# A token mixer behind linear attention: three groups of transfers moved in the program

## The chip, the cores and the metric

The kernel runs on one core of one Trainium2 chip. The metric is device time in microseconds (us), the median of five runs. Beside it there is one profiled execution, whose trace gives each instruction's start and length on each engine: TensorE (PE; PEld is its loading of weights), VectorE (DVE), ScalarE (ACT), GpSimd (POOL), and SyncE (SP), which only issues transfers.

## The reference

For each of 8 batches, 8 heads, 576 tokens and head size 64:

```
phi(x) = elu(x) + 1
kv  = phi(k)^T v                      # 64 x 64 for each head
x   = phi(q) kv / (phi(q) . sum(phi(k)) + 1e-6)     # heads side by side: 576 x 512
h   = relu(x^T w_tok1) w_tok2         # mixes the tokens: 512 x 576
u   = x + h^T
out = u + relu(u w_ch1) w_ch2         # mixes the channels: 512 -> 1536 -> 512
```

Inputs and output are float32; the products run on bf16 operands.

## The kernel before

A batch's 576 tokens are four tiles of 128 and a tail of 64. The tails of two batches (an even one and the odd one after it) are worked on together. The main loop works in blocks: block n does the channel mixer of batch n on TensorE (mm3 against w_ch1 at L543, then w_ch2) and, in between, everything that batch n + 1 and n + 2 need: phi of q and k, kv, the attention quotient (nd_all, L261), mm1 and mm2 of the token mixer.

The order on every engine is the program's own order; no scheduler changes it. Each block has a list `big` of TensorE steps and a list `fill` of other work, each with the number of the step behind which it is put: `put(24, phi_end, "k", 3, 2, 2)` puts this work behind step 24. Entries of one number keep the order in which they were put. An engine carries out its own instructions in that order and waits at each for what it needs, so an instruction that waits holds up all behind it on the same engine.

The names that matter here:

- `phi_exp`, `phi_add`, `phi_end` (L151, L157, L165): exp on ScalarE; max(x + 1, 1), called y, on VectorE; then their minimum on VectorE into `qp` or `kp`. Each runs twice for a batch, on half of the heads.
- `qtr_dma` (L219 to 223): SyncE transposes `qp` into `qT` with two transposing transfers, one for each half of the partitions. `utr_dma` (L519) does it for two tiles of `u` at a time, `utr_tail_dma` for the tails. `live["crossbar"]` remembers the last such transfer of q or u.
- `mm2a`, `mm2b` (L325): the second product of the token mixer for tiles 0, 1 and for 2, 3. VectorE adds x (L337); that is u. `uta` and `utb` are the two transfers that transpose u into uT.
- `load_all(n, nms, gate)` (L916): SyncE loads of a batch. With a gate, the first load waits until the given transfer has landed.
- `kv` (L191, then copies on ScalarE at L197).
- The product with w_ch2 is one step of Strassen's scheme in Winograd's form: seven products of half the size (`pair_product`, L854; in the last block `product`, L768, and `tail_product`, L823 for the pair of tails), with sums of rows beforehand (`row_sums`, L655) and sums of results in PSUM. `pair_end` (L863) reads a result and adds u. `mix_one` (L712) does the same to a part of mm3; its results pass an add and relu on VectorE (L531). `pair_copy` (L859) keeps a partial result on ScalarE. `mm4` for the tails (L583) is direct.
- `group_sums` (L700) and `u_sums` (L689) are the sums of weights and of uT for these schemes; `mm4_end` (L610) reads the result of a pair of tails.
- `last_block` follows a string `SEQUENCE`: `p61` is product 6 of half j = 1 with its read, `P61` the product alone, `R61` the read alone; `t6` is product 6 of the tails with its read, `T` and `U` product and read alone; `s` are the tails' row sums on GpSimd. Reads are L778 and, for the tails, L833.

Outputs leave through obuf. In the blocks before the last, GpSimd issues them (L869, and L612 for tails). In the last block SyncE and ScalarE do: the second half j = 1 in quarters of 64 KB for each issue (L798), the first half j = 0 in two issues of 256 KB when its last quarter is done (L801), the tails in four issues of 128 KB (L837), two of which are GpSimd's.

There are eight semaphores for the transfers that SyncE and ScalarE issue, used in turn; an issue first waits until the last transfer on its semaphore has landed. In the last block the two engines issue alternately, so that is the transfer four places back on the same engine.

Of the kernel before, what the change touches and what calls it, by code (L numbers as in the profile page):

```python
# [19 lines left out]
def kernel(  # L20
# [20 lines left out]
    nc = tc.nc  # L41

    B, H, S, D = q.shape
# [3 lines left out]
    R = 4  # L47
# [66 lines left out]
    half = [slice(0, 64), slice(64, 128)]  # L114
# [28 lines left out]
    def o_slots(m):  # L143
        at = o_at[0] if o_at[0] + m <= 8 else 0
        o_at[0] = (at + m) % 8
        return obuf[:, at:at + m]
# [69 lines left out]
        for h, ts in enumerate(TS):  # L216
            qtr_put(n, c, ts, tp[:, h], put)

    def qtr_dma(n):  # L219
        for a in range(2):  # L220
            live["crossbar"] = nc.sync.dma_start_transpose(
                out=qT[n % 2][:, 2 * TD * a:2 * TD * (a + 1)].rearrange("p (f s) -> p f s", s=D),
                in_=qp[half[a]].rearrange("p c t i d -> p (c t i d)"))
# [365 lines left out]
    outv = out.rearrange("n (p t) d -> n p t d", t=T)  # L589
# [163 lines left out]
    HC = [slice(0, 256), slice(256, 512)]  # L753
# [17 lines left out]
    def product_read(n, j, i):  # L771
        b = n % 2
        ps = live[{2: "Z", 5: "Y", 3: "Y"}.get(i, "X"), j]
        if i == 1:
            live["oj", j] = o_slots(2)
        o = live["oj", j]
        ur = lambda e, c: u[b][:, 2 * j + e, HC[c]]
        add = lambda e, c, x_, y_: nc.vector.tensor_tensor(out=o[:, e, HC[c]], in0=x_, in1=y_,  # L778
                                                           op=ALU.add)
        if i == 1:  # L780
            add(0, 0, ps, ur(0, 0))
        elif i == 2:
            add(0, 0, ps, o[:, 0, HC[0]])
        elif i == 6:
            add(0, 1, ps, ur(0, 1))
        elif i == 5:
            add(1, 1, ps, ur(1, 1))
        elif i == 7:
            add(1, 1, ps, o[:, 1, HC[1]])
        elif i == 4:  # L790
            add(1, 0, ps, ur(1, 0))
        elif i == 3:
            add(0, 1, ps, o[:, 0, HC[1]])
        queues = [nc.sync, nc.scalar]
        if j == 1 and i in (2, 7, 3, 4):
            d, cs = {2: (0, HC[0]), 7: (1, HC[1]), 3: (0, HC[1]), 4: (1, HC[0])}[i]
            for e in range(2):
                queues[e].dma_start(out=outv[n, :, 2 * (2 * j + d) + e, cs], in_=o[half[e], d, cs])  # L798
        elif i == 4:
            for e in range(2):  # L800
                queues[e].dma_start(out=outv[n, :, 4 * j + e:4 * j + e + 3:2], in_=o[half[e]])  # L801

# [21 lines left out]
    def tail_read(i):  # L826
        ps = live["t", {1: 2, 2: 7, 5: 3, 3: 3}.get(i, 2)]
        if i == 1:
            live["ot"] = o_slots(2)
        o = live["ot"]  # L830
        e, c, x_ = {1: (0, 0, ut[0]), 2: (0, 0, None), 6: (0, 1, ut[0]), 5: (1, 1, ut[1]),
                    7: (1, 1, None), 4: (1, 0, ut[1]), 3: (0, 1, None)}[i]
        nc.vector.tensor_tensor(out=o[:, e, HC[c]], in0=ps,  # L833
                                in1=o[:, e, HC[c]] if x_ is None else x_[:, HC[c]], op=ALU.add)
        if i in (3, 4):
            for b, queue in enumerate((nc.sync, nc.scalar) if e else (nc.gpsimd, nc.gpsimd)):
                queue.dma_start(out=outv[B - 4 + 2 * e + b, :, 2 * R], in_=o[half[b], e])  # L837


    ORDER = [1, 2, 6, 5, 7, 3, 4]  # L840
# [26 lines left out]
    def pair_put(n):  # L867
# [6 lines left out]

    SEQUENCE = """m01 m02 m11 m05 m15 m06 m12 c0 m21 m03 m16 m07 c1 m25 m13 m22 m17 m04 c2 m26 m14
        m23 c3 m27 r0 c4 m24 r2 c5 T10 T20 T11 T21 r4 s P10 R10 P20 P11 P50 U1 U2 R11 P60 R60
        P21 R50 P70 R20 R70 P51 R21 R51 p30 p61 p40 t6 t5 p71 t7 t3 t4 p31 p41"""

    def last_block(n):
        for e in SEQUENCE.split():  # L880
# [246 lines left out]
    put = lambda s, fn, *a: fill.append((s, lambda: fn(*a)))  # L1127
# [33 lines left out]
    put(19, todo["mm2a"])  # L1161
    put(19, todo["uta"])
    put(20, pair_copy, 1)
    put(20, phi_end, "k", 3, 0, 2)
    put(22, pair_copy, 2)
    put(22, phi_exp, "k", 3, 2, 2)
    put(22, vcast, 3, 1)
    put(24, phi_end, "k", 3, 2, 2)
    put(24, pair_end, 1, "X", 1, 1, 2)
    put(24, todo["mm2b"])  # L1170
    put(24, todo["utb"])
    put(24, pair_end, 1, "Z", 0, 0, 0)
    put(27, lambda: load_all(4, "qkv", live["crossbar"]))
    put(26, pair_end, 1, "Y", 0, 1, 1)
    put(28, pair_end, 1, "X", 1, 0)
    put(28, pair_put, 1)
    put(28, group_sums)
    put(28, kv, 3, range(2))
    run(big, sorted(fill, key=lambda e: e[0]))

    MIXED = (2, 3, 4, 5, 6)
    for n in range(2, B - 1):
        p, b = divmod(n, 2)
        tail = int(n == 3)
        mix = n in MIXED
        big = (m3x if mix else m3)(n) + m3t * tail + m4s(n) + m4(p, [8]) * tail
        b0 = 12 + 3 * tail
        todo = dict(steps(n + 1))
        fill = []
        put = lambda s, fn, *a: fill.append((s, lambda: fn(*a)))  # L1190
        at = lambda s, *nms: [put(s, todo.pop(nm)) for nm in nms if nm in todo]

        def phi_at(nm, ex, ad, en):
            for g in range(2):
                if ex is not None:
                    put(ex[g], phi_exp, nm, n + 2, 2 * g, 2)
            for g in range(2):
                put(ad[g], phi_add, nm, n + 2, 2 * g, 2)
                put(en[g], phi_end, nm, n + 2, 2 * g, 2)

        at(1, "nd")
        if mix and 3 < n < B - 2:
            for which in (3, 4):
                put(2, u_sums, which, tuc, b)
        if n + 2 < B:
            if n > 3:
                phi_at("k", None, (2, 2), (3, 4))
                put(5, load_all, n + 3, "k")
            nm = "k" if n == 3 else "q"
            if n > 3:  # L1210
                phi_at(nm, (7, 7), (10, 10), (16, 16))
            else:
                for which in (3, 4):
                    put(3, u_sums, which, tuc, b)
                for g in range(2):
                    put(3, phi_add, nm, n + 2, 2 * g, 2)
                    put(7, phi_exp, nm, n + 2, 2 * g, 2)
            put(16 if n > 3 else 10,
                *((qtr_dma, n + 2) if n != 3 else (load_all, n + 3, "k")))
            if n == 2:  # L1220
                for g in range(2):
                    put(13, phi_add, "k", n + 2, 2 * g, 2)
        at(7, "mm1")
        for s, k0 in ((7, 0), (11, 3)):
            for w in (1, 2):
                put(s, row_sums, n, w, k0, 3)
        if n < 4:
            for g in range(2):
                put(7 + 2 * g, phi_end, nm, n + 2, 2 * g, 2)
        if mix:  # L1230
            for which in (1, 2):
                put(0, u_sums, which, tuc, b)
        if n == 3:
            phi_at("q", (12, 13), (13, 13), (14, 14))
            put(15, qtr_dma, n + 2)
        at(13, "mm2a", "uta")
        put(14, row_sums, n, 3, 0, KH)
        put(b0 + 1, pair_copy, 0)
        if n == 2:
            for g in range(2):  # L1240
                put(b0 + 1, phi_exp, "k", n + 2, 2 * g, 2)
                put(b0 + 2, phi_end, "k", n + 2, 2 * g, 2)
            put(b0 + 4, load_all, n + 3, "k")
        at(b0 + 3 - tail, "mm2b", "utb")
        put(b0 + 4 - tail, row_sums, n, 4, 0, KH)
        put(b0 + 4 - tail, pair_end, n, "Z", 0, 0, 0)
        put(b0 + 5, pair_copy, 1)
        if n + 2 < B:
            for g in range(2):
                put(b0 + (5 if n == 2 else 2) + g, vcast, n + 2, g)  # L1250
        if n != 2:
            put(b0 + 7, lambda: load_all(n + 3, "qv", live["crossbar"] if n > 3 else None))
        put(b0 + 7, pair_copy, 2)
        if n > 2 and n + 3 < B:
            put(b0 + 8, k_exp, n + 3)
        put(b0 + 9, pair_end, n, "X", 1, 1, 2)
        if n == B - 2:
            at(b0 + 6, "mm2t", "utt")
        at(b0 + 9, "mm2t")
        if n + 2 < B:  # L1260
            put(b0 + 9, kv, n + 2, range(2))
        at(b0 + 9, "utt")
        if n == 2:
            put(b0 + 9, load_all, n + 3, "qv")
        put(b0 + 11, pair_end, n, "Y", 0, 1, 1)
        if n == B - 2:
            for which in (3, 4):
                put(3, u_sums, which, tuc, b)
            put(1, first_sum)
            for which in range(1, 5):  # L1270
                if which > 1:
                    put((3, 3, b0 + 2)[which - 2], first_sums, which)
                put(b0 + 10, u_sums, which)
        else:
            put(b0 + 13, pair_end, n, "X", 1, 0)
            put(b0 + 13, pair_put, n)
        assert not todo, todo
        run(big, sorted(fill, key=lambda e: e[0]))
# [31 lines left out]
```

## Time and profile before

| | |
|---|---|
| time, median of 5 runs | 250.85 us (248.11 to 251.35) |
| profiled execution | 251.13 us, of which the span from the first to the last instruction is 249.4 us |
| granted TensorE clock | 0.998 |
| PE busy | 236.6 us (95%) |
| DVE busy | 197.5 us (79%) |
| ACT busy | 139.3 us (56%) |
| POOL busy | 78.5 us (31%) |
| HBM read, written | 35.85 MB, 9.44 MB |

The profile names a group of instructions by the line of the program and what it writes and reads. "Busy" leaves out waiting and issuing. A row of waits reads: who waited, at which line, for whom, then the sum in us, how many times, and the longest. The chain of work that ended last is followed from the last instruction back to what released it. A stretch's row in a table of windows gives the stretch, its length, each engine's busy time with the number of its instructions, the granted clock, the share of the transfer engines that was busy, and GB/s.

### The profile page before, as it was taken

The page shows a single profiled execution, that of the slowest core. Times are in us where ns is not written, and L with a number is a line of the kernel's source. Part 1 is how long each engine was busy: PE and PEld are TensorE (multiplying, and loading weights), DVE is VectorE, ACT ScalarE, POOL GpSimd, SP SyncE. Part 2 cuts the span into 40 slices and gives each one's busy share as a digit, 9 for nine tenths or more (in the row PEclk, how much of TensorE's full clock was granted, in tenths as well). Part 3 has the DMA queues.
Part 4 walks back from the last instruction along what each step waited for, and adds up shares of the span by engine and source line. Part 5 has one row for each costly group of instructions (what it writes and reads, how often), then busy time and mean ns, then how long its engine had stood idle before and what let it go on. Part 6 is the DMA issues. An engine that isn't in the chain of part 4 may idle for free.

```text
span 249.4 us, 6065 instructions
## 1 busy us (share of the span) xinstructions
PE 236.6 (95%) x2476; PEld 162.2 (65%) x2496; DVE 197.5 (79%) x349; ACT 139.3 (56%) x224; POOL 78.5 (31%) x90
## 2 busy tenths in 40 slices
PE   7799999999999898989999999999999999999992
PEld 3484455554877455755688556775677566888881
DVE  5954878897999768997995489978996879956862
ACT  4764791579765276735897168556853651266000
POOL 9770030496504500062002600061006700520551
PEclk9999999999999999999999999999999999999999
DMA  6999999999525699669948975357929702361045
GB/s 247 266 203 258 359 260 335 329 277 300 226 54 114 125 315 355 141 175 355 345 142 139 356 257 189 65 119 257 314 51 131 168 3 42 63 135 36 3 103 152
DMA packets 49708, 48.40 MB, mean 194 GB/s; under 512 B 30032, under 2 KB 35536, under 8 KB 49680
## 3 DMA queue, kind: packets, MB, share of 16 engines
q1 hardware_dynamic: 41568, 34.87, 46.6%
q0 software_dynamic: 7568, 12.49, 22.9%
q10 hardware_dynamic: 544, 0.66, 0.9%
q8 instruction: 19, 0.31, 0.5%
q14 instruction: 9, 0.07, 0.1%
HBM read 35.85 MB, written 9.44 MB: 182 GB/s over the span
## 4 chain that ended last, share of the span: by engine, by line
PE 53%; DMA 8%; DVE 7%; issue 2%; DVEq 0%
PE ps L854 15%; PE ps L543 12%; PE ps L712 5%; DMA q_raw<-in_q_dram 4%; DMA uT<-u 4%; PE ps L740 4%; PE ps L768 4%; PE ps L312 3%; PE ps L325 3%; PE ps L570 2%; PE ps L823 2%; DVE u L337 1%; PE ps L261 1%; DVE v_raw L655 1%; DVE y L157 1%
## 5 line engine op out<-in xcount | busy, mean ns | idle before, releaser
L543 PE MATMUL ps<-uT,wc 128*128 128x512 bf16 x252 | 60.2, 379 | 2.1 <-DMA uT<-u 1.8
L550 ACT ACTIVATE cr<-ps 128x512 bf16<-128x512 f32 x59 | 34.5, 600 | 34.6 <-PE ps L543 34.5
L543 PEld LDWEIGHTS <-wc 128*128 128x128 bf16 x256 | 24.0, 98 | 26.8 <-DMA uT<-u 2.5
L865 POOL TENSOR_TENSOR obuf<-obuf,q_raw 128x512 f32<-128x512 f32 x6 | 7.6, 1269 | 96.7 <-DVE obuf L863 63.2
L854 PE MATMUL ps<-k_raw,v_raw 128*128 128x256 bf16 x216 | 24.9, 273 | 0.0
L854 PEld LDWEIGHTS <-cr 128*128 128x128 bf16 x216 | 20.9, 98 | 5.2 <-DVE cr L531 1.5
L854 PEld LDWEIGHTS <-v_raw 128*128 128x128 bf16 x216 | 21.1, 98 | 3.9 <-issue 0.4
L151 ACT ACTIVATE e<-q_raw 128x1152 bf16<-128x1152 f32 x16 | 18.5, 1163 | 8.3 <-DVE den L241 5.2
L863 DVE TENSOR_TENSOR obuf<-ps,u 128x512 f32<-128x512 f32 x24 | 16.1, 685 | 7.2 <-PE ps L854 5.0
L151 ACT ACTIVATE e<-k_raw 128x1152 bf16<-128x1152 f32 x16 | 18.2, 1165 | 3.5 <-DMA k_raw<-in_k_dram 3.5
L854 PE MATMUL ps<-wc,cr 128*128 128x256 bf16 x144 | 17.9, 273 | 1.2 <-DVE cr L531 1.2
L276 DVE TENSOR_TENSOR x<-ps,dens 128x768 bf16<-128x768 f32 x18 | 17.2, 954 | 0.4
L655 DVE TENSOR_TENSOR v_raw<-cr 128x768 bf16<-128x768 bf16 (+2 forms) x24 | 14.8, 617 | 1.6 <-ACT cr L718 1.6
L337 DVE TENSOR_TENSOR u<-ps,x 128x1024 bf16<-128x1024 f32 x12 | 14.6, 1219 | 0.7 <-PE ps L325 0.3
L157 DVE TENSOR_SCALAR y<-q_raw 128x1152 bf16<-128x1152 f32 x16 | 11.9, 767 | 2.9 <-DMA q_raw<-in_q_dram 2.9
L176 ACT CAST vs<-v_raw 128x1152 bf16<-128x1152 f32 x12 | 13.5, 1161 | 0.0
L157 DVE TENSOR_SCALAR y<-k_raw 128x1152 bf16<-128x1152 f32 x16 | 11.7, 763 | 2.1 <-DMA k_raw<-in_k_dram 2.1
L312 PE MATMUL ps<-x,w 128*128 128x512 bf16 x49 | 13.0, 379 | 0.3
L165 DVE TENSOR_TENSOR qp<-e,y 128x1152 bf16<-128x1152 bf16 x16 | 11.7, 753 | 0.9 <-ACT e L151 0.6
L865 POOL TENSOR_TENSOR obuf<-obuf,part 128x512 f32<-128x512 f32 x6 | 7.6, 1271 | 14.3 <-DVE obuf L863 14.3
L325 PE MATMUL ps<-ar,w2p 128*128 128x512 bf16 x44 | 11.8, 379 | 0.3
L583 PE MATMUL ps<-wc,cr 128*128 128x512 bf16 x47 | 11.8, 379 | 0.2 <-DMA wc<-in_moe_w_ch_dram 0.2
(183 smaller groups left out, 465.9 us busy)
## 6 DMA issues: line engine op xcount, KB each, us to landing
k_raw<-in_k_dram SPq DMA_DIRECT2D x16, 576.0 KB, 6.2
q_raw<-in_q_dram SPq DMA_DIRECT2D x16, 576.0 KB, 6.4
v_raw<-in_v_dram SPq DMA_DIRECT2D x14, 576.0 KB, 9.6
out_dram<-obuf POOLq DMA_DIRECT2D x12, 512.0 KB, 6.5
wc<-in_moe_w_ch_dram POOLq DMA_DIRECT2D x8, 384.0 KB, 10.0
out_dram<-obuf POOLq DMA_DIRECT2D x4, 256.0 KB, 5.2
out_dram<-obuf POOLq DMA_DIRECT2D x6, 128.0 KB, 6.1
cr<-in_v_dram POOLq DMA_DIRECT2D x2, 288.0 KB, 7.6
```

Of the source, the lines that this page charges most:

```text
L151: nc.scalar.activation(out=e, in_=f, func=AF.Exp)
L157: nc.vector.tensor_scalar(out=y, in0=f, scalar1=1.0, scalar2=1.0, op0=ALU.add, op1=ALU.max)
L276: nc.vector.tensor_tensor(out=xv[:, :, rc0:rc0 + 3], in0=v_[m][:, :, k0:k0 + 6, 0:D].rearrange("p i (q a) d -> p i q a d", a=2), in1=den.r ...
L312: nc.tensor.matmul(out=ps[:, mt], lhsT=w1t[:, b, ms] if r == R else w1[:, r, ms], rhs=x[b][:, r, :], start=(r == 0), stop=(r == R))
L325: nc.tensor.matmul(out=ps[:, i], lhsT=w2v(kt, r, b), rhs=ar[b][:, kt, :], start=(kt == 0), stop=(kt == NT - 1 and not add))
L337: nc.vector.tensor_tensor(out=u[b][:, rs[0]:rs[0] + m], in0=ps[:, 0:m], in1=x[b][:, rs[0]:rs[0] + m], op=ALU.add)
L543: nc.tensor.matmul(out=ps, lhsT=wc1[:, kj, 128 * mc:128 * mc + 128], rhs=uTj[b][:, kj] if n < 2 else uT[b][:, :, kj], start=(kj == 0), sto ...
L550: nc.scalar.activation(out=cr[b][:, mc, :], in_=ps, func=AF.Relu)
L655: return engine.tensor_tensor(out=s_[which - 1][:, ks], in0=x_, in1=y_, op=op)
L854: nc.tensor.matmul(out=live[tile_][:, j], lhsT=lhs[:, k_], rhs=rhs[:, k_], start=(first and j == 0 and k_ == 0), stop=(k_ == KH - 1), skip ...
L863: nc.vector.tensor_tensor(out=o, in0=live[tile_], in1=u[n % 2][:, d::2, HC[c]], op=ALU.add)
L865: nc.gpsimd.tensor_tensor(out=o, in0=o, in1=part[i], op=ALU.add)
```

## The change

Three places change. The line numbers of all that stands behind them move by one to three.

1. **Block 1, batch 3's k and kv.** The two `phi_end` of batch 3's k, behind steps 20 and 24 so far, both go behind step 25. In the order of VectorE they stood between batch 2's first and second u; now they stand behind the second u and one more `pair_end`. `kv` of batch 3 goes from step 28 to step 31, which is behind the twelve matmuls of the tails' `mm4` (L583) instead of ahead of them.
2. **Blocks 4 and 5, q of batches 6 and 7.** `phi_end` of q goes from step 16 to step 10, right behind its `phi_add`. `qtr_dma` gets a second argument. Its first transfer goes to step 10 and stands on SyncE's queue ahead of the two of u; its second stays at step 16, behind them.
3. **The last block.** The first half's output too leaves in quarters, each as soon as it is done, and so do the tails', all of them from SyncE and ScalarE. SyncE and ScalarE then issue twelve outputs each in place of six, and GpSimd none in place of two. In the sequence the tails' products 6, 5, 7, 3 and 4 move ahead; which products are done, and the last two (`p31 p41`), stay.

```diff
-    def qtr_dma(n):
-        for a in range(2):
+    def qtr_dma(n, halves=range(2)):
+        for a in halves:
...
-        if j == 1 and i in (2, 7, 3, 4):
+        if i in (2, 7, 3, 4):
             d, cs = {2: (0, HC[0]), 7: (1, HC[1]), 3: (0, HC[1]), 4: (1, HC[0])}[i]
             for e in range(2):
                 queues[e].dma_start(out=outv[n, :, 2 * (2 * j + d) + e, cs], in_=o[half[e], d, cs])
-        elif i == 4:
-            for e in range(2):
-                queues[e].dma_start(out=outv[n, :, 4 * j + e:4 * j + e + 3:2], in_=o[half[e]])
...
-        if i in (3, 4):
-            for b, queue in enumerate((nc.sync, nc.scalar) if e else (nc.gpsimd, nc.gpsimd)):
-                queue.dma_start(out=outv[B - 4 + 2 * e + b, :, 2 * R], in_=o[half[b], e])
+        if i in (2, 7, 3, 4):
+            for b, queue in enumerate((nc.sync, nc.scalar)):
+                queue.dma_start(out=outv[B - 4 + 2 * e + b, :, 2 * R, HC[c]],
+                                in_=o[half[b], e, HC[c]])
...
-        P21 R50 P70 R20 R70 P51 R21 R51 p30 p61 p40 t6 t5 p71 t7 t3 t4 p31 p41"""
+        P21 R50 P70 R20 R70 P51 R21 R51 t6 t5 p30 t7 p40 p61 t3 t4 p71 p31 p41"""
...
-    put(20, phi_end, "k", 3, 0, 2)
...
-    put(24, phi_end, "k", 3, 2, 2)
     put(24, pair_end, 1, "X", 1, 1, 2)
     put(24, todo["mm2b"])
     put(24, todo["utb"])
+    for g in range(2):
+        put(25, phi_end, "k", 3, 2 * g, 2)
     put(24, pair_end, 1, "Z", 0, 0, 0)
...
-    put(28, kv, 3, range(2))
+    put(31, kv, 3, range(2))
...
             if n > 3:
-                phi_at(nm, (7, 7), (10, 10), (16, 16))
+                phi_at(nm, (7, 7), (10, 10), (10, 10))
...
-            put(16 if n > 3 else 10,
-                *((qtr_dma, n + 2) if n != 3 else (load_all, n + 3, "k")))
+            if n > 3:
+                put(10, qtr_dma, n + 2, [0])
+                put(16, qtr_dma, n + 2, [1])
+            else:
+                put(10, *((qtr_dma, n + 2) if n != 3 else (load_all, n + 3, "k")))
```

## The prediction

> **What bounds the kernel now.** I read the busy shares, then the chain that ended last in order of time, then TensorE's waits, then windows cut at those waits. TensorE is busy 236.6 of 249.4 us at a granted clock of 0.998, so only its gaps are worth anything. Its waits from 66 us on are these:
>
> ```profile
> PE ps L543 <- DMA uT<-u: 1.8, 2, 1.0
> PE ps L854 <- DVE cr L531: 1.2, 1, 1.2
> ```
>
> Windows cut there (stretch, length, then TensorE's busy time first) show that after 111.51 us nothing is left to win on TensorE before the last 4.9 us:
>
> ```profile
> 82.95:83.67 0.72, 0.00 (x0) 0.00 (x0) 0.72 (x2) 0.00 (x0) 0.72 (x2) 1.00 0.00 0
> 97.30:98.50 1.20, 0.03 (x1) 0.03 (x2) 1.20 (x3) 0.54 (x2) 0.00 (x0) 1.00 0.99 390
> 110.50:111.51 1.01, 0.00 (x0) 0.00 (x1) 0.73 (x2) 0.00 (x0) 0.95 (x2) 1.00 1.07 379
> 111.51:244.50 132.99, 132.47 (x1341) 96.68 (x1350) 107.41 (x190) 70.73 (x113) 34.38 (x37) 1.00 0.58 157
> ```
>
> Three gaps, 0.72 + 1.19 + 1.03 = 2.94 us (the longest waits, unrounded), and the chain (start, length, what) ties them together:
>
> ```profile
> 77.83 1.13 DVE u L337
> 78.96 0.03 DVE obuf L863
> 78.99 4.64 DMA uT<-u
> 83.63 0.05 issue
> 83.67 0.47 PE ps L543 x2
> 84.14 10.56 DMA q_raw<-in_q_dram
> 94.71 0.02 issue
> 94.73 0.03 DVE y L157
> ...
> 105.42 1.13 DVE u L337
> 106.55 0.03 DVE q_raw L655
> 106.58 4.88 DMA uT<-u
> ```
>
> Batch 2's second u is late, its transfer takes 4.64 us, and the gate on batch 4's q loads (they wait for the last transposing transfer) passes that on: the q loads leave at 83.68 and 84.14 and land only at 94.71, VectorE stands in front of y, and everything behind y on its queue (the add-and-relu of L531, batch 3's u) is late. That makes the second gap, and through batch 3's u the third.
>
> Why 4.64 us? The twelve u transfers take 3.0/3.2/5.6 us (min/median/max). In the DMA view of 78.9 to 83.7 us, 40 slices of 0.12 us, the packets are over by slice 22 (81.7 us), but one more queue is at work:
>
> ```profile
> DMA  0000000000199999999994500000000000000000
> q1 hardware_dynamic: 1056, 0.26, 29.1%
> q8 instruction: 1, 0.02, 1.3%
> ```
>
> [...] I read the row so: one 16 KB instruction packet (1.3% of 16 engines over 4.8 us, 1.0 us on one) stood in one engine's way. [...] The same packet stands in the window of the 4.88 us transfer.
>
> **Part 1: batch 2's u sooner.** VectorE runs in order. Before: u 74.67, two kp of 1.42 together to 77.23, X's obuf 77.15 to 77.83, second u from 77.75. The two L165 now stand behind X, u and Z. TensorE's mm2b ends at 76.93, the product before it about 75.9; so X runs to about 76.75 and u from 76.97 to 78.18: 0.78 sooner, not the 1.42 of the kp, because mm2b is late next. SyncE waits only for this u, so the transfer leaves at 78.21. Moved work: kp now ends near 80.4, Y and the last X follow (81.6), then L700 (2.6) and L610 near 84.9, some 0.7 to 1.0 later than before (L610 ended at 83.88). L610 must empty bank 2 before nd_all, which TensorE reaches near 84.8: I charge 0.15. kv needs kp at 80.4, but kv itself is moved behind L583 (2.76 from 79.47) to 82.2, so kp is covered by 1.8; without the move of kv TensorE would stand 0.9. ScalarE's kvbd copies (0.77) follow, before nd_all at 84.9.
>
> The transfer lands between 81.3 (3.1) and 82.85 (4.64). TensorE is ready at 82.95. So the 0.72 gap goes at either price. What differs is when q's loads leave: 81.4 or 82.9. The instruction packet came 2.2 us after kv's start; with kv (144 instructions) behind L583 that place in TensorE's stream is passed near 82.9, and even at the old 81.63 it comes after the packets' end. I take 3.1.
>
> GpSimd's output writes go out at 82.61 and land up to 9 us later. In before, q followed them by 1.07 us and took 9.6 and 10.56. In the next block q left at 111.19, 1.08 us ahead of such writes (112.27), and took 5.1 and 8.2. After the change q leaves 81.4 and 81.8, about 1.1 us ahead: the nearest row says landings at 86.5 to 90.0. The other bound is the old 10.6: 92.4. VectorE reaches y at 91.03 - 0.45 = 90.6, so by the nearest row it doesn't wait. Then by the old durations: the L531 of product 7 at 92.2, when its part copy on ScalarE is there (was 95.41); the L531 of products 2 and 3 at 94.75 and 95.4 (was 97.73, 98.33); TensorE comes for them at 97.28 - 0.55 = 96.73 and does not wait: the 1.19 gap goes. Batch 3's u ends about 103.95 (was 106.55, 2.6 sooner); its transfer lands at 107.1, or 108.85 with a packet in its way; TensorE gets there at 110.48 - 1.72 = 108.76. The third gap costs 0 to 0.1. Sum of part 1: 2.94 - 0.15 = 2.8 less.
>
> **Part 2: q's transfers of batches 6 and 7 around u's.** No TensorE gap stands in these blocks, so it can gain nothing there; what can it lose? In block 4, qp (two L165, 1.42 together) moves ahead of row sums 1 and 2 and both u. By the old timeline: y and qp 154.29 to 156.96, row sums to 158.07; product 6 needs them at 158.84: 0.77 to spare. Row sum 3 ends 160.15, product 7 needs it at 161.5. u ends 159.2 and 161.3 (was 158.1, 160.27). On SyncE's queue the first q half (1.34) leaves at 157.0 and is issued by 158.4, ahead of u's; the second stands behind both u. uT lands at 161.3 + 3.2 = 164.5, or 166.1 with a packet in the way; L543 needs it at 166.76. Block 5 is the same 25.3 us later (182.25, 183.35 against 184.10; 189.8 or 191.4 against 191.46). q landed at 168.36 against nd_all's 168.58; it now lands before 166.5. The gated q and v loads start up to 2 us sooner and meet the same writes; their readers had slack. Cost 0; from both sides -0.1 to +0.6 for the two blocks, should a u transfer take its worst 5.6.
>
> **Part 3: outputs of the last block.** TensorE's 11 last products keep their sum of 0.655 each. t6 now starts at 237.06; GpSimd's sums run from 233.66, 1.64 each, the second ending 237.02: up to 0.1 of wait. t7 needs 238.6, comes at 239.0; t3 needs 240.2, comes at 241.0. Out go two GpSimd writes (issued 243.22 and 243.77, landed 2.8 later in the median) and two 256 KB pairs; SyncE and ScalarE now issue 12 writes of 64 KB each. The end before, with the issue of each write (start, length):
>
> ```profile
> 243.63 0.50 ACTq L837 DMA_DIRECT2D out_dram<-obuf  x1
> 244.29 1.95 ACTq L798 DMA_DIRECT2D out_dram<-obuf  x2
> ```
>
> The last product ends at 244.46, its read at 244.91, the last issue at 246.24, the landing near 248.2, and closing takes 1.2. Each queue waits with a write until its write four places back has landed. For the last that is t3's, issued near 242.35; at the 3.1 of the 64 KB rows it lands at 245.4, half a us after the last read. Without GpSimd's writes beside it, the issue may fall from 1.07 to the 0.5 of the other rows. So: landing 245.4 + 2.5 to 3.1, that is 247.9 to 248.5, against 248.2. [...] I take 0, between -0.6 and +0.4.
>
> **Sum.** The profiled execution took 251.13 us, span 249.4 plus 1.7 outside. Less 2.8: 248.35; it lies 0.28 over the median of 250.85, so about 248.1 for the median. One of the five runs of before took 248.11, 2.74 under the median: just the three gaps. I take that as a run whose transfers met no packet, an inference and no measurement.
>
> **The rivals.**
> - A, as summed (chance 0.57): 248.1, between 247.2 and 248.9. For it: the row of 111.19. Against it: it hangs on a lead of 1.1 us over the writes.
> - B, q still meets the writes (0.30): u's transfer is slow again (82.85), or the writes slow q all the same. Then VectorE's chain moves by only 0.8 and gaps two and three stay beside it: 250.85 - 0.8 = 250.0. For it: 10.56 us where loads start behind writes.
> - C, slower (0.07): the last block's 12 writes per queue. The last landing is t3's issue plus two latencies, 242.35 + 2L. At L = 3.0 it is the old end; the gain of 2.8 is gone at L = 4.4; at L = 4.8 (the 512 KB outputs take 6.5 in the median) the time is 248.1 + 3.75 = 251.9, and a full per cent slower from L = 5.5. Against it: a pair of 64 KB writes each 0.655 us is 200 GB/s, and slices of the end before moved up to 363.
> - D, the change does not do what it says (0.06): another wait, L610 or part 2's u, eats the gain: about 250.9.
>
> **How the numbers follow.** The predicted time is A's. Eight in ten: from A's lower bound 247.2 into B up to 250.5; C and the worst of D stay out. One per cent (2.5 us, to 248.34) is about what a measurement of this kernel can tell from no change. A lies on both sides of it, some three quarters under it: faster 0.45. The rest of A, B, D and the milder half of C: 0.50. The rest of C with a little of D: 0.05.
>
> **What would show it.** In the profile after: the second u ending near 78.2, no wait of L543 for uT near 83, q loads issued near 81.5 with landings of 5 to 9 us, no wait of L854 for L531, batch 3's u near 104, gapless TensorE through blocks 4 and 5, last landing within half a us of 3.7 after the last product. Wrong would be: q landing after 92, a packet in batch 2's u transfer, or the last issue later than 1 us after the last read.

## The result, and the profile after

The kernel after takes 247.57 us in the median of 44 runs (247.03 to 248.72), the kernel before 250.77 us in the 79 runs set beside it. The ratio is 0.9911, 95% interval 0.9892 to 0.9929: faster by 0.9%. It is formed from the runs within 1.5% of their kernel's fastest, low and high ones of before together, and so is nearer to 1 than the quotient of the two medians, 0.987. The forecast was 248.1, between 247.2 and 250.5. The profiled execution took 248.03 us with a span of 246.3 (before 251.13 and 249.4).

One thing has to be known for all that follows. The 79 times of before lie in two groups: 22 of them between 247.49 and 248.44 (median 247.83), 57 between 250.19 and 252.20 (median 250.84), none in between. The clock does not tell them apart: in the 55 runs of before beside the first experiments it was 0.995 to 1.000 in both. The profiled execution of before belongs to the upper group. After has one group. So after is 3.3 us under before's upper group and 0.3 us under its lower one: nearly all of the gain lies in the runs that fell into the upper group.

TensorE's waits from 66 us on, in the profile of after:

```profile
PE ps L261 <- DVE obuf L610: 0.6, 1, 0.6
PE ps L543 <- DMA uT<-u: 0.3, 1, 0.3
```

The three waits of before, 2.94 us, are gone; 0.62 us at L261 near 85 us and 0.25 us at L543 at 189.45 us have come. The stretch from 75 to 109 us in the timeline of after (start, length, engine, line):

```profile
77.23 1.22 DVE L337 TENSOR_TENSOR u<-ps,x 128x1024 bf16<-128x1024 f32 x1
...
78.97 2.49 DVE L165 TENSOR_TENSOR kp<-e,y 128x1152 bf16<-128x1152 bf16 x2
79.13 1.71 POOL L863 TENSOR_TENSOR obuf<-obuf,q_raw 128x512 f32<-128x512 f32 x1 [0.59 <-DVE obuf L861]
...
81.59 0.88 SPq L132 DMA_DIRECT2D q_raw<-in_q_dram  x2
...
83.05 1.90 PE L543 MATMUL ps<-uT,wc 128*128 128x512 bf16 x8
...
83.70 1.26 POOL L867 DMA_DIRECT2D out_dram<-obuf  x2 [0.30 <-DVE swc L700]
...
84.74 0.68 DVE L610 TENSOR_TENSOR obuf<-ps,ut 128x512 f32<-128x512 f32 x1
85.57 0.80 PE L261 MATMUL ps<-kvbd,qT 64*128 64x65 bf16 x40 [0.62 <-DVE obuf L610]
...
91.01 1.42 DVE L157 TENSOR_SCALAR y<-q_raw 128x1152 bf16<-128x1152 f32 x2
...
103.37 1.22 DVE L337 TENSOR_TENSOR u<-ps,x 128x1024 bf16<-128x1024 f32 x1
...
109.09 1.89 PE L543 MATMUL ps<-uT,wc 128*128 128x512 bf16 x8
```

The reader is to see the order: u ends at 78.45, q's loads leave at 81.59, 2.1 us ahead of GpSimd's writes of 83.70, and y and L543 have no wait behind them. L543 of block 3 starts at 109.09 instead of 111.51. The DMA view of the same 78.9 to 83.7 us, where before had an instruction packet, has none: its only queue is this one, and the first run of slices is u's transfer (issued 78.48, landed 81.53).

```profile
DMA  0000003999999999920000000000003498938999
q1 hardware_dynamic: 1161, 0.50, 51.4%
```

The end, as rows of the windows (stretch, length, then TensorE's busy time first), TensorE's last product ending at 242.48:

```profile
111.70:242.50 130.80, 130.05 (x1293) 95.00 (x1302) 106.20 (x187) 69.42 (x111) 31.66 (x33) 1.00 0.59 157
242.50:246.30 3.80, 0.00 (x0) 0.00 (x0) 0.42 (x1) 0.00 (x0) 0.00 (x0) 0.98 0.51 117
```

and the last issues in the timeline:

```profile
242.48 1.26 ACTq L798 DMA_DIRECT2D out_dram<-obuf  x2
242.51 0.42 DVE L778 TENSOR_TENSOR obuf<-ps,u 128x256 f32<-128x256 f32 x1 [0.25 <-PE ps L768]
242.97 0.48 SPq L798 DMA_DIRECT2D out_dram<-obuf  x1
```

From the end of the last product to the end of the span it is 3.79 us; in before it was 4.91. The last landing is at 245.20. The page's list of issues says why (KB each, median us to landing):

```profile
out_dram<-obuf ACTq DMA_DIRECT2D x12, 64.0 KB, 2.2
out_dram<-obuf SPq DMA_DIRECT2D x12, 64.0 KB, 1.9
```

So the span is 2.0 us shorter in TensorE's stream and 1.1 us shorter at the end, together 3.1: 249.4 to 246.3.

### The profile page after: what moved, and what is told of

It is laid out like the page before. It is cut to its first block, busy times and chain, and to the rows that moved or that the text cites. A ratio compares the mean times of both kernels' runs of the same rounds, so it can differ in the third digit from the quotient of the medians.

```text
span 246.3 us, 6090 instructions
## 1 busy us (share of the span) xinstructions
PE 237.1 (96%) x2477; PEld 162.5 (66%) x2496; DVE 198.5 (81%) x349; ACT 139.3 (57%) x224; POOL 76.9 (31%) x88
## 4 chain that ended last, share of the span: by engine, by line
PE 84%; DVE 6%; DMA 5%; issue 2%; ACT 1%; SPq 0%; DVEq 0%
PE ps L543 22%; PE ps L852 18%; PE ps L712 6%; PE ps L312 6%; PE ps L583 5%; PE ps L740 4%; PE ps L768 4%; PE ps L325 4%; DMA q_raw<-in_q_dram 3%; PE ps L557 2%; PE ps L570 2%; DMA uT<-u 2%; PE ps L820 2%; PE ps L261 2%; PE ps L191 1%
## 5 line engine op out<-in xcount | busy, mean ns | idle before, releaser
L543 PE MATMUL ps<-uT,wc 128*128 128x512 bf16 x252 | 60.2, 380 | 0.6 <-DMA uT<-u 0.3
L550 ACT ACTIVATE cr<-ps 128x512 bf16<-128x512 f32 x59 | 34.7, 600 | 32.6 <-PE ps L543 32.5
L543 PEld LDWEIGHTS <-wc 128*128 128x128 bf16 x256 | 24.1, 98 | 24.8 <-issue 0.6
L165 DVE TENSOR_TENSOR qp<-e,y 128x1152 bf16<-128x1152 bf16 x16 | 11.9, 754 | 1.7 <-ACT e L151 1.0
L165 DVE TENSOR_TENSOR kp<-e,y 128x1152 bf16<-128x1152 bf16 x16 | 12.7, 816 | 0.5 <-ACT e L151 0.4
L583 PE MATMUL ps<-wc,cr 128*128 128x512 bf16 x47 | 11.8, 379 | 0.1
```

The source lines that it names most:

```text
L165: live["phi"] = nc.vector.tensor_tensor(out=dst.transpose([0, 2, 1, 3]), in0=e.rearrange("p (i t d) -> p i t d", i=nj, t=T), in1=y.rearran ...
L543: nc.tensor.matmul(out=ps, lhsT=wc1[:, kj, 128 * mc:128 * mc + 128], rhs=uTj[b][:, kj] if n < 2 else uT[b][:, :, kj], start=(kj == 0), sto ...
L550: nc.scalar.activation(out=cr[b][:, mc, :], in_=ps, func=AF.Relu)
L583: nc.tensor.matmul(out=ps, lhsT=crt[:, kc, :] if t == 8 else cr[b][:, kc, 128 * r:128 * r + 128], rhs=wc2[:, kc, :], start=(kc == 0), stop ...
```

## The experiments

My theory was that of the prediction: q's loads of batch 4 lose five us when they go out behind GpSimd's writes of batch 1; u's transfer, slow because of an instruction packet, is what put them there; the last block is worth nothing. The rivals were that u's own time is what counts, that the writes slow q in any order, and that the gain lies in the last block.

### The three parts alone

**Part 1 alone** (block 1's edit, nothing else):

```diff
-    put(20, phi_end, "k", 3, 0, 2)
-    put(24, phi_end, "k", 3, 2, 2)
+    for g in range(2):
+        put(25, phi_end, "k", 3, 2 * g, 2)
-    put(28, kv, 3, range(2))
+    put(31, kv, 3, range(2))
```

> Part 1 alone (batch 3's two phi_end of k behind batch 2's second u, kv behind L583). Theory, q's loads get ahead of GpSimd's writes: the three gaps near 83, 98 and 111 us go, L610 costs 0.6 as in the changed kernel, so 2.2 to 2.7 us less than a run of before with its gaps, about 248.3, and the upper group of times of before (250.2 to 252.2) is empty. Rival, the gain is only that u is 0.8 us sooner: 250.0, and times stay in two groups.

Measured: 248.74 us (248.35 to 249.08), one group, ratio 0.9984 (0.9955 to 1.0013). Against the median of before made beside it, 250.46, it is 1.7 less; against before's upper group it is 2.1 less, against its lower group 0.9 more. A ratio to a kernel with two groups depends on how many of its runs fall into which: here 26 of 55 were low. TensorE's wait:

```profile
PE ps L261 <- ACT cr L550: 0.6, 1, 0.6
```

The three gaps are gone and 0.6 us at L261 is there, as in after (the view puts it down to ScalarE's L550 here and to L610 there).

**Part 2 alone** (the q transfers of blocks 4 and 5):

```diff
-                phi_at(nm, (7, 7), (10, 10), (16, 16))
+                phi_at(nm, (7, 7), (10, 10), (10, 10))
...
+                put(10, qtr_dma, n + 2, [0])
+                put(16, qtr_dma, n + 2, [1])
```

> Part 2 alone (q's transposing transfers of batches 6 and 7 around u's). Theory: no gap of TensorE is touched, so the time is that of before within 0.3 us in either of its two groups (about 250.8 and 247.8); TensorE waits at most 0.4 us for uT in block 6. Rival, moving the transfers apart is what brings the gain: under 248.5 in all runs.

Measured: 249.36 us in the middle of two groups, ten times in 247.53 to 248.29 and ten in 250.44 to 252.0; ratio 0.9986 (0.9942 to 1.003). These are before's two groups: part 2 does nothing that can be measured, and it does not touch what makes the groups. Its profile fell into the lower group and shows what before does there: u's transfer takes 3.05 us (79.45 to 82.50), q's loads leave at 82.55, 0.53 ahead of the writes at 83.08, and land at 86.43 and 88.98. There is no TensorE wait from 66 us on. In this profile the instruction packet moves at 89.3.

**Part 3 alone** (the last block):

```diff
-        if j == 1 and i in (2, 7, 3, 4):
+        if i in (2, 7, 3, 4):
...
-        if i in (3, 4):
+        if i in (2, 7, 3, 4):
...
-        P21 R50 P70 R20 R70 P51 R21 R51 p30 p61 p40 t6 t5 p71 t7 t3 t4 p31 p41"""
+        P21 R50 P70 R20 R70 P51 R21 R51 t6 t5 p30 t7 p40 p61 t3 t4 p71 p31 p41"""
```

> Part 3 alone (last block's outputs in quarters from SyncE and ScalarE, tails' products ahead). Theory from the two traces: from the last product's end to the end of the span 3.8 us where before had 4.9, so 0.9 to 1.1 us less in each group: about 249.8 and 246.8. My prediction's reckoning of a wait four places back: 0, that is 250.8 and 247.8.

Measured: 246.83 us (246.59 to 246.94), ratio 0.9878 (0.9804 to 0.9952). There are four runs, and all fell into the lower group; the profile has u's transfer as in the run above. Part 3 changes nothing ahead of the last block, so I take that for chance (with 26 low runs in 55, four in a row come about once in twenty times). It is to be read against before's lower group, 247.83: 1.0 less. From the last product to the end of the span it takes 3.80 us. This was the first sign that the last block is worth 1 us and not nothing.

### What part 1 does

**q behind the writes again.** After, with one thing undone: batch 4's loads wait for the last sum of L700 and so leave behind GpSimd's writes. u stays as early as in after.

```diff
-            nc.vector.tensor_tensor(out=swc[:, o], in0=x_, in1=y_, op=op)
+            live["gs"] = nc.vector.tensor_tensor(out=swc[:, o], in0=x_, in1=y_, op=op)
...
-    put(27, lambda: load_all(4, "qkv", live["crossbar"]))
...
     put(28, group_sums)
+    put(28, lambda: load_all(4, "qkv", live["gs"]))
```

> The changed kernel with one wait more: batch 4's q loads wait for the last of the four L700 instead of for the transposing transfer, and so leave about 1.1 us behind GpSimd's writes, as in before; all else as in the changed kernel, u and kv too. Theory: q lands 9 to 11 us after its issue, VectorE stands before y until about 95, L852 waits for L531 by 1 to 1.5 us, and the third gap is back by up to 1 us: 1.2 to 2.5 us more than the changed kernel, 248.8 to 250. Rival, u's 0.8 us are what counts: within 0.3 us of the changed kernel, 247.6.

Measured: 250.68 us (250.18 to 251.76), 3.1 over after; ratio to before 1.005 (1.002 to 1.008). TensorE's waits:

```profile
PE ps L852 <- DVE cr L531: 1.3, 1, 1.3
PE ps L543 <- DMA uT<-u: 0.9, 1, 0.9
PE ps L712 <- DVE cr L531: 0.9, 1, 0.9
PE ps L261 <- ACT cr L550: 0.6, 1, 0.6
```

The chain that ended last, in order of time:

```profile
85.35 10.55 DMA q_raw<-in_q_dram
95.91 0.02 issue
95.93 0.03 DVE y L157
95.97 0.64 issue
96.61 0.68 DVE cr L531
...
106.62 1.14 DVE u L337
107.76 0.03 DVE q_raw L655
107.78 4.78 DMA uT<-u
```

q's loads left at 84.89 and 85.35, 1.2 us behind the writes of 83.71, and landed 9.5 and 10.6 us later. They left 3.3 us later than in after and landed 8.7 us later, so some 5.4 us come from their place behind the writes. Before's second and third gap are back, with an early and undisturbed u (transfer 78.49 to 81.55). u's own time is not what counts.

**The writes behind q.** The converse on before: GpSimd's writes of batch 1 wait until q's second load of batch 4 has landed; u and kv stay as they were.

```diff
-                    load(nm, n, g, gate)
+                    live["load", nm, n, g] = load(nm, n, g, gate)
...
-            nc.gpsimd.dma_start(out=outv[n, :, e:e + 7:2], in_=live["o4"][half[e]])
+            after(nc.gpsimd.dma_start(out=outv[n, :, e:e + 7:2], in_=live["o4"][half[e]]),
+                  live["load", "q", 4, 1] if n == 1 and e == 0 else None)
```

> The kernel before, with batch 1's output writes on GpSimd waiting until batch 4's second q load has landed; nothing else is changed, u and its transfer least of all. Theory, loads behind writes are what costs: an instruction packet in u's transfer then costs only the first gap of 0.7 us, since q no longer meets writes; runs at 247.8 (no packet) and about 248.5 (packet), none over 249.3. Rival, the slow transfer of u itself carries the loss: the upper group stays at 250.5 to 251.

Measured: 248.21 us (247.22 to 249.48), ratio 0.9979 (0.9934 to 1.0024). Twelve runs, none in the upper group, though two lie over the 249.3 that I had given as the highest. In the profile q lands 3.4 and 4.5 us after its issue, the writes leave at 87.56, and no TensorE wait is left. It does not test the packet: in its profile u's transfer took 3.05 us. But with the writes held back no run paid for three gaps.

**kv alone, and the phi_end alone.** Part 1 has two moves. First before with kv behind L583 only:

```diff
-    put(28, kv, 3, range(2))
+    put(31, kv, 3, range(2))
```

> The kernel before with kv of batch 3 moved behind L583 and nothing else; batch 2's u is not sooner. Theory, the packet is asked for at a place in TensorE's stream: that place is now passed 2 us or more later, after u's transfer has landed, so there is one group of times only, 247.6 to 248.2. Rival, the packet comes at a time that kv doesn't move: two groups, about 247.8 and 250.8.

Measured: 248.07 us (247.8 to 248.85), 20 runs, one group; ratio 0.997 (0.994 to 0.9999). There is no TensorE wait from 66 us on. The timeline of this run, where u's transfer is issued at 79.20, as late as in before:

```profile
79.20 1.23 SPq L521 DMA_TRANSPOSE uT<-u  x1
...
82.31 0.88 SPq L132 DMA_DIRECT2D q_raw<-in_q_dram  x2
...
82.83 1.26 POOL L869 DMA_DIRECT2D out_dram<-obuf  x2 [0.30 <-POOL obuf L865]
```

The lead of q over the writes is 0.52 us, and it is enough: q lands at 86.12 and 88.67. The DMA view of 78.9 to 83.7 us shows one queue alone, and no instruction packet:

```profile
DMA  0000000000003999999999920000000000006384
q1 hardware_dynamic: 1077, 0.31, 34.7%
```

kv itself starts at 82.50, behind L583. So moving kv removes the upper group without moving u.

Then before with the two phi_end moved only (the first four lines of part 1's diff).

> The kernel before with batch 3's two phi_end of k behind batch 2's second u, kv left where it was. From the changed kernel's trace, where the two L165 take 2.5 us beside GpSimd's additions and end at 81.4: kv (L191), which TensorE reaches at 79.5, waits 1.5 to 2.0 us for them, everything behind it is late by that, and the wait of L261 goes; q still leaves early, so no other gap: 249.3 to 250.2 in one group. By the prediction's reckoning kp ends at 80.4 and the wait is 0.9: 248.5 to 249.

Measured: 249.39 us (248.8 to 249.95), 20 runs, one group; ratio 0.9998 (0.9967 to 1.0028). TensorE's only wait from 66 us on:

```profile
PE ps L191 <- DVE kp L165: 1.3, 1, 1.3
```

The upper group is gone here too, and TensorE stands 1.25 us for kp where I had reckoned 0.9. This run makes u sooner and holds kv up at once, so it does not tell which of the two emptied the upper group. What it does tell, beside the others, is a price: part 1 with both moves takes 248.74 and kv's move alone 248.07. As the change was made, moving the two `phi_end` costs 0.7 us, and the wait at L261 is 0.6 of it.

**Where the 0.6 us at L261 comes from.** After, with L700 behind L610 on VectorE, so that L610 no longer queues behind L700:

```diff
-    put(28, group_sums)
+    put(31, group_sums)
```

> The changed kernel with the four L700 (group_sums) moved from step 28 to step 31, behind the read of the tails (L610). Theory, L261 waits 0.6 us for L610, which stands behind the L700: the wait goes, 0.4 to 0.7 us less than the changed kernel, about 247.0, below the lower group of before (247.4 to 248.4). Rival, L261 waits for ScalarE's reads beside it: no change, 247.6.

Measured: 246.64 us (246.25 to 247.42), 20 runs; ratio 0.9895 (0.9866 to 0.9924). No TensorE wait is left from 66 us on. The median is 0.9 us below after's and the lowest of all the kernels with more than four runs. Of the 0.9, the L261 wait is 0.62; the 0.25 at 189 us is missing from this profile too, which the edit does not aim at.

### What part 3 does

These four stand on parts 1 and 2 with the edit just shown; none of their times falls into the upper group.

**The old last block.**

```diff
-        if i in (2, 7, 3, 4):
+        if j == 1 and i in (2, 7, 3, 4):
...
+        elif i == 4:
+            for e in range(2):
+                queues[e].dma_start(out=outv[n, :, 4 * j + e:4 * j + e + 3:2], in_=o[half[e]])
...
-        P21 R50 P70 R20 R70 P51 R21 R51 t6 t5 p30 t7 p40 p61 t3 t4 p71 p31 p41"""
+        P21 R50 P70 R20 R70 P51 R21 R51 p30 p61 p40 t6 t5 p71 t7 t3 t4 p31 p41"""
```

> Parts 1 and 2 with the L700 behind L610, the last block as in before. From the end of the last product to the last landing 3.7 us as in before: 1.0 us more than the same kernel with part 3 (e8, 246.6), so 247.6. By my prediction's reckoning of part 3 (worth 0): 246.6.

Measured: 247.88 us (247.57 to 248.26, 4 runs), ratio 0.9899 (0.9841 to 0.9956). From the last product to the end of the span it takes 4.78 us, and the last landing comes 3.58 after the last product. Against the run with all three parts (246.64) part 3 is worth 1.2 us. And against kv's move alone (248.07) all the rest of parts 1 and 2, u's 0.8 us included, is worth 0.2 us once the wait at L261 is out of the way.

**Only the new order of the products, the outputs as in before.**

```diff
-        P21 R50 P70 R20 R70 P51 R21 R51 p30 p61 p40 t6 t5 p71 t7 t3 t4 p31 p41"""
+        P21 R50 P70 R20 R70 P51 R21 R51 t6 t5 p30 t7 p40 p61 t3 t4 p71 p31 p41"""
```

> As e9, with the new order of the last products and the old outputs (GpSimd's two and the 256 KB pairs stay). Theory, the last writes were slow because the tails' four writes, GpSimd's among them, were still moving: with t3 and t4 two places earlier half or more of the 1.0 us comes, 246.8 to 247.2. Rival, only the size and the queue of the writes count: 247.6.

Measured: 249.13 us (248.56 to 250.02, 20 runs), ratio 0.9982 (0.9952 to 1.0013): 1.3 slower than with the old order, where I had expected a gain. From the last product to the end of the span it takes 6.14 us. The issues of its last 10 us, the first five rows (KB each, median us to landing):

```profile
out_dram<-obuf SPq DMA_DIRECT2D x1, 256.0 KB, 3.3
out_dram<-obuf ACTq DMA_DIRECT2D x1, 256.0 KB, 4.4
out_dram<-obuf POOLq DMA_DIRECT2D x2, 128.0 KB, 4.8
out_dram<-obuf SPq DMA_DIRECT2D x3, 64.0 KB, 4.5
out_dram<-obuf ACTq DMA_DIRECT2D x3, 64.0 KB, 4.5
```

The same 64 KB that take 1.9 to 2.2 us in after take 2.9 to 4.8 here, behind 256 KB and 128 KB transfers issued from 238.2 to 240.3 us. The 1.3 us themselves lie in the issuing. A row of the timeline from 242.8 us on:

```profile
241.69 2.51 ACTq L798 DMA_DIRECT2D out_dram<-obuf  x2
```

The first of these two issues takes 1.86 us, so the last write leaves 1.97 us behind the last product, where it left 0.71 behind it with the old order. It then lands 2.92 us later, as with the old order (2.88). Why an issue takes so long is open.

**Only the new outputs, the order as in before.**

```diff
-        if j == 1 and i in (2, 7, 3, 4):
+        if i in (2, 7, 3, 4):
...
-        if i in (3, 4):
-            for b, queue in enumerate((nc.sync, nc.scalar) if e else (nc.gpsimd, nc.gpsimd)):
-                queue.dma_start(out=outv[B - 4 + 2 * e + b, :, 2 * R], in_=o[half[b], e])
+        if i in (2, 7, 3, 4):
+            for b, queue in enumerate((nc.sync, nc.scalar)):
+                queue.dma_start(out=outv[B - 4 + 2 * e + b, :, 2 * R, HC[c]],
+                                in_=o[half[b], e, HC[c]])
```

> As e9, with the new outputs (quarters, SyncE and ScalarE alone) and the old order of the products. Theory, crowding: t7, t3, t4 still finish just ahead of the last two, but in quarters, so part of the 1.0 us comes: 246.9 to 247.3. Rival, GpSimd's writes alone are the cause: all of it, 246.6. My prediction's wait four places back would show here as a wait of the last issue for a landing.

Measured: 246.68 us (246.58 to 246.81, 4 runs), ratio 0.985 (0.9794 to 0.9906); 3.82 us from the last product to the end of the span, the last writes landing 1.92 to 2.24 us after their issue. The last issue leaves 0.69 us behind the last product, so there is no wait four places back. That is part 3's whole gain, as the rival had it; the next run tests the rival's reason. The new order adds nothing to it, and without the new outputs it costs 1.3.

**GpSimd or size?** The new outputs, but the quarters of the tails' first two results (`t2`, `t3`) go out by GpSimd, as their 128 KB did in before.

```diff
-            for b, queue in enumerate((nc.sync, nc.scalar)):
+            for b, queue in enumerate((nc.sync, nc.scalar) if e else (nc.gpsimd, nc.gpsimd)):
```

> As e8, with the two tail quarters of the even batch (t2 and t3) issued by GpSimd again in place of SyncE and ScalarE; order and sizes as in the changed kernel. Rival, GpSimd's way of writing slows the last issues (1.07 and 1.26 us in before against 0.5): the last issue is 0.5 or more longer again and 0.4 to 1.0 us are lost, 247.0 to 247.6. Theory, crowding alone: at most 0.2 us, 246.6 to 246.8.

Measured: 247.04 us (246.39 to 247.52, 4 runs), ratio 0.9855 (0.9786 to 0.9925). By its median it falls into the rival's range, but the end of its profile (247.52) does not: 3.92 us from the last product to the end of the span, 0.15 more than without the edit, and GpSimd's 64 KB landed 2.05 to 2.58 us after their issue. This execution was already 0.8 us behind at batch 2's second u transfer (issued at 78.92, against 78.09 without the edit). So that GpSimd issues is not what made the old end long. What remains, by elimination, is the size of the pieces still in flight when the last one is issued. No run separates the tails' 128 KB from the first half's 256 KB, but in the profile of the old last block the 256 KB have landed at 240.76 and the last issue leaves at 241.70, while the four of 128 KB land from 242.02 to 243.72.

## Why the prediction was right, step by step

**The base was one of two groups.** I took the one time of 248.11 among before's five as a run whose transfers met no packet, "an inference and no measurement". It is now measured: part 2 alone and part 3 alone were both profiled at a low time, with u's transfer of 3.05 and 3.06 us, the packet at 89.3 and 88.6, after q's loads had left, and no TensorE wait. In the profile of kv's move it comes at 88.9.

That the packet holds the transfer up, as the prediction read it, can be seen in the packets of before. Of the transfer's 1056 packets all but two have begun when the instruction packet starts at 81.63; the last two begin when it ends, at 82.59 and 82.60. The view of 81.7 to 83.6 us has these two alone:

```profile
q1 hardware_dynamic: 2, 0.00, 0.1%
```

The 14 profiles (before, after and the twelve runs) hold 168 transfers of u. The 19 in which an instruction packet began and ended took 4.64 to 5.62 us, the other 149 took 3.02 to 3.41. Among the 149 are 12 that such a packet met in their last 0.6 us, and none of their own packets began behind it.

What the runs don't settle is what decides when the packet comes. The queue carries 19 packets of 16 KB in the profiles of before and of after. A request at a place in TensorE's stream, the theory put ahead of the run of kv's move, would agree with all three single groups that moved kv or delayed it (kv's move, the phi_end's move, both). But in the profile of part 2 TensorE's stream is that of before, no packet of any queue moves from 82.15 to 83.5 us, and the instruction packet still comes only at 89.3. So the place alone does not decide it: what sets the packet's time, and with it the group that a run falls into, stays open.

**Part 1.** The order of events was right, and nearly every size:

| step | predicted | measured |
|---|---|---|
| second u ends | 78.18 | 78.45 |
| u's transfer | 3.1 | 3.05 |
| q's issues | 81.4, 81.8 | 81.59, 82.05 |
| q's lead over the writes | 1.1 | 2.1 |
| q's landings | 86.5 to 90.0 | 85.66, 87.14 |
| y starts | 90.6 | 91.01 |
| L531 of product 7 and of 2, 3 start | 92.2, 94.75, 95.4 | 92.85, 95.21, 95.82 |
| batch 3's u ends | 103.95 | 104.59 |
| kp ends | 80.4 | 81.46 |
| L610 ends | 84.9 | 85.42 |
| wait at L261 | 0.15 | 0.62 |

mm2b itself came 0.27 later in this execution, so the first row is exact. Two sizes were off, by one cause. I charged the two L165 at 1.42 us together, the row of their old place. In the new place they took 2.49:

```profile
L165 DVE TENSOR_TENSOR kp<-e,y x2: 748/1286/1823, 79.0 to 79.6; 128x1152 bf16<-128x1152 bf16 x2
```

(min/median/max in ns: the first took 748, the second 1823). Beside them GpSimd's addition of 79.13 took 1.71 us instead of the 1.27 of its neighbours, and the second L165 ends 0.6 us behind it. In their old place no GpSimd instruction ran. The other 30 L165 of this profile and the 32 of before, none of them beside an addition of GpSimd's, took 0.74 to 0.76 us each; in the run of the phi_end alone the two stood beside an addition of 1.71 us again and took 2.48 together. That the second L165 and the addition held each other up is my reading of these rows. I looked at VectorE's queue and not at what GpSimd does in the window into which the work moves. The same price is the 1.25 at kv in the run of the phi_end alone, where I wrote 0.9. The delay passed to GpSimd too: its writes went out at 83.70 and not at 82.61, which is why q's lead was 2.1 and not 1.1. There the error helped.

What I gave as part 1's mechanism, u sooner, is not needed for the gain. The gaps go because the packet leaves u's transfer and q gets ahead of the writes, and kv's move alone does both. I had named the packet's place behind kv, but as a reason for 3.1 us and not as the main effect. The move of the `phi_end`, which makes u sooner, costs 0.7 as it was made; with the wait at L261 taken out, u's 0.8 us and all else of parts 1 and 2 is worth 0.2.

**Part 2.** Predicted 0 between -0.1 and +0.6, measured 0 in the run of part 2 alone. In after one u transfer of block 5 met an instruction packet (4.93 us from 184.47) and TensorE stood 0.25; in the run with the new order alone it was 5.15 us and 0.5. Both lie within the 0.6 that I had named for it.

**Part 3: the step that failed.** I wrote "I take 0, between -0.6 and +0.4". It is -1.0 (alone, against the lower group) to -1.2 (with and without it, parts 1 and 2 the same). The term that was wrong is the latency of a 64 KB write at the very end, "2.5 to 3.1" from the median rows of before. It was 1.9 to 2.2: the very last write left 0.71 us behind the last product in both kernels and took 3.02 us in before, 2.01 in after. The sign that I had set, 3.7 us give or take half from the last product to the last landing, was missed with 2.72. The rows of before were taken beside 128 KB and 256 KB writes in flight, which the change itself takes away. The -0.6 rests on a term for the last write that no run shows; what the runs showed in its place is the 1.9 to 2.2 us. The wait four places back, on which I had the last landing at 247.9 to 248.5, did not arise either: t3's writes landed at 242.26 and 242.54, before the last issues at 242.97 and 243.19.

**The sum.** Predicted -2.8 and 0. In the two spans it is -2.94 + 0.62 + 0.25 = -2.07, and -1.12 at the end: -3.2 against 3.1 in the spans. Two errors of size, +0.7 in TensorE's waits and -1.1 at the end, lie against each other, and by that luck the forecast is nearer (0.5 us) than its steps are. It also rests on before's median lying in the upper group, as it did with 57 of 79 runs.

**The rivals.** B, that q still meets the writes, is what happens when it is made to: 250.68 in the run with q held back, against the 250.0 that I gave it. B's first half, that the writes slow q all the same, fell with a lead of half a us (kv's move alone). C, late landings from twelve writes in a queue, fell: L was 2, not 4.4. D has a small part: L610 ate 0.6.

## What to carry to other kernels

When times fall into two groups with nothing between, look for two transfers that race, and for what is gated on the one that can lose: here half a us of lead over other writes decided over five us of landing time and 3 us of kernel. Before work is moved on one engine, look at what the other engines do in the new window, and charge the neighbours' price and not that of the old place: the two L165 took 2.49 us beside GpSimd's addition and 1.42 where no GpSimd instruction ran. Here the last outputs were better cut small and sent as they came, with nothing large in flight beside them. And take a change of several moves apart even when it gains: one of these moves cost 0.7 us.

## What was not expected of the hardware

- An instruction packet of 16 KB cost a transposing transfer 1.6 us (4.64 against 3.05), because two of its 1056 packets began only when that packet had ended, and with what is gated on that transfer 3 us of the kernel. At 88.6 to 89.3 us, with q's loads in flight, it cost TensorE nothing.
- Loads of 576 KB issued half a us to 2 us ahead of GpSimd's writes land in 3.8 to 6.0 us (q's two loads in after and in the runs of part 2 and of kv alone), the same loads 1.1 to 1.6 us behind them in 9.5 to 10.6. The writes take 8.6 to 10.1 us in the one order and 4.4 to 8.5 in the other.
- An order of products that changes no output's size can cost 1.3 us: with the old outputs in the new order each write issued from 239.8 to 241.7 us took 4.5 to 5.1 us to land, the 64 KB ones included, and issues of 0.5 us took up to 1.9. Two instruction packets of another queue (8 KB each, at 240.9 and 243.6 us) lie in that stretch; whether they have a part in it is open.
